# A spectral mixing layer with a cosine-gated MLP on one core: the order of the opening's transfers, and two weight columns fetched through DRAM

## The chip, the cores and the metric

The kernel runs on one core of one Trainium2 chip. The metric is the device time of one execution in microseconds (us). The core's engines are named as in the profile: PE (TensorE, matrix products), DVE (VectorE), ACT (ScalarE), POOL (GpSimd) and SP (SyncE, which here only issues transfers). Everything is in 32-bit floats.

## The reference

`x` has 8 batches of 3008 rows with 256 columns. `w_in` is 256 x 2048 and `w_out` is 2048 x 256.

```
X   = fft(x, over the 3008 rows); X = fft(X, over the 256 columns); a = real(X)
h   = a @ w_in              # 24064 rows, 2048 hidden columns
out = (h * cos(h)) @ w_out
```

## The kernel before, in words

**The transform.** 3008 is 47 x 64. The transform over the rows is made in two stages: a first stage over 47 (`first_half` for the first batch, `pair_half` for the others), whose result `z` is written to DRAM (`store_z`, `store_pair`) and read back in another layout (`load_z`), and a second stage (`second_half`, with the table `BJ`). The transform over the 256 columns is folded into `w_in`: `weights(e, q)` multiplies a quarter q of `w_in` with a cosine (e = 0) or sine (e = 1) table, and `keep_weights` copies the result to `WC` or `WS`. `mix_weights` forms the sums and differences of the raw rows of `w_in` that this needs.

**The row that becomes columns.** The sine of frequency zero is zero, so row 0 of `WS` is free and carries the weights of the alternating column. For each quarter n of the hidden columns, these 512 numbers are needed as four columns of 128, in `wn[:, 4n:4n+4]`. `turn_wn(n)` makes them on PE with four products that have one row and one column (L634), and then has POOL set the row of `WS` to zero (L642). `keep_wn(n)` has DVE copy them out (L645). They are read by `seed` (L694, on ACT), which starts each hidden block's accumulator with `nb * wn + 0.25`; block f of 16 reads column f. So quarter 1 serves blocks 4 to 7, quarter 2 blocks 8 to 11 and quarter 3 blocks 12 to 15.

**The steps.** A step is one batch, one group of about 256 row frequencies (225 in the first group) and one pair of hidden blocks: 8 x 6 x 8 = 384 steps of two halves each. The main loop runs over passes k; pass k starts half k, and does the second product of the step that lies five passes back. In a pass, in this order as far as the opening is concerned:

- `mm1(half, 0)` and `mm1(half, 1)` (L713): the products with `WC` and `WS`; between them ACT copies out the first (`act_e`, L725), and behind them DVE forms the mirrored half (`dve_h`, L729).
- `act_round` (L741, ACT), `dve_frac` (L745, DVE), `act_sin` (L751, ACT), `dve_g` (L755, DVE): h * cos(h), spread over the next passes.
- `sums` (L771, L777, L778, POOL) at pass 2d + 3: sums of the parts of step d, in a tile `S`.
- `mm2` (L804): seven products of step d in place of eight, with blocks of `w_out` and with sums of such blocks. The first three (two with `w_out` itself, one with a sum) come in pass 2d + 5, the fourth at the end of it, the last three in pass 2d + 6.

The sums of blocks of `w_out` are made by POOL in `combine_w2(f0, f1)` (L679, four instructions per pair of blocks) into the tile `VX`. Rows of `w_out` are loaded by `load_w2(f0, f1)` (L254), a quarter (512 KB) at a time. The first step needs the first quarter, (0, 2).

**The opening.** Until the weights are ready, PE makes the first stage of the first batch, and fillers (`keep_busy`, L659). The last six `weights` come within passes 0 to 4. `turn_wn` and `keep_wn` for the quarters 1, 2 and 3 come in passes 1, 3 and 5. What is loaded and combined in which step stands in the dictionary `opening`.

**The queues.** The order on each engine is the order of the program, written out by hand. SP issues nearly all transfers, in its order. In the built program the transfers that SP issues carry eight semaphores in turn, so that each of them waits, before it is issued, for the landing of the one eight places ahead. Two quarters of `w_out`, (0, 2) and (2, 4), are issued by POOL instead, behind its work of pass 1. SP's order around the change, before: the third and fourth quarter of `w_in` with two transfers of `store_z` between them; four more of `store_z`; `load_w2(4, 6)`; `load_bj(256, 512)`; `load_w2(6, 8)`; eight of `load_z` (columns 4 to 8 of z, 32 KB each); the table `L2`; then the second batch's `x`.

**The second batch's x.** `transform(1)` schedules it by steps: `turn_x` (L187, L192; a reversed copy from DRAM to DRAM) in steps 0 and 1, `load_xx` (L210, L217) in steps 1 to 4. POOL reads it first in `take_middle` (L370) from step 8 on.

Of the kernel before, what the change touches and what calls it, by code (L numbers as in the profile page):

```python
# [11 lines left out]
FP = mybir.dt.float32  # L12
# [119 lines left out]
def kernel(  # L132
# [106 lines left out]
    def load_w(q, eng=nc.sync, i0=0, i1=2):  # L239
        eng.dma_start(  # L240
            out=wr[q][:, 512 * i0 : 512 * i1].rearrange("p (i f) -> p i f", f=512),
            in_=moe_w_in[128 * i0 : 128 * i1, 512 * q : 512 * q + 512].rearrange(
                "(i p) f -> p i f", p=128
            ),
        )

    def load_bj(c0, c1, eng=nc.sync):
        eng.dma_start(out=BJ[:, c0:c1], in_=B_dr.ap()[:, c0:c1])
# [4 lines left out]
    def load_w2(f0, f1, eng=nc.sync):  # L253
        eng.dma_start(  # L254
            out=w2.rearrange("p (q c) -> p q c", c=ND)[:, 2 * f0 : 2 * f1],
            in_=moe_w_out.rearrange("(q p) c -> p q c", p=128)[:, 2 * f0 : 2 * f1],
        )
# [210 lines left out]
    def store_z(p, j0=0, j1=NJ, engs=(nc.sync, nc.sync)):  # L468
        half, q = divmod(p, 2)
        zd, zs = take_zd(0, half), zps[p][:, 0:1024]  # L470
        for e in range(2):
            p0 = 16 * e + XP * q
            engs[e].dma_start(
                out=zd[p0 : p0 + XP, 256 * j0 : 256 * j1].rearrange("i (y d) -> y i d", d=128),
                in_=zs[64 * e + 2 * j0 : 64 * e + 2 * j1, :].rearrange("y (i d) -> y i d", d=128),
            )
# [88 lines left out]
    def transform(b):  # L565
        todo = {}

        def at(o, *call):
            todo.setdefault(o, []).append(call)

        for p in range(4):
            sh = (3, 3, 3, 0)[p] if b == 1 else 0
            o = 8 * p + sh
            if p < 2:
                at(p, turn_x, b, p)
            at(1 + p, load_xx, b, p)
            at(5 + p + (3 if b == 1 else 0), take_middle, b, p)
            for k in range(2):
                at(o + 6 + k, fold_x, b, p, k)
                at(o + 9 + k, fold_z, b, p, k)  # L580
            pairs[per * (b - 1) + o + 9] = b, p
            at(o + 11, patch_z, b, p)
            at(o + 12, store_pair, b, p)
            if p == 0:
                for e in range(2):
                    at(4 + 2 * sh + e, fold_ends, e)
                middles.add(per * (b - 1) + o + 10)
                at(o + 12, store_ends, b)
        at(23, load_z, b, 0)
        at(39, load_z, b, 1)  # L590
        for i in range(3):
            doubles[per * (b - 1) + (44, 46, 47)[i]] = b, (2 * i, 2 * i + 1)
        return todo
# [37 lines left out]
    def turn_wn(n, pw):  # L631
        for k in range(4):
            f = 512 * n + 128 * k
            nc.tensor.matmul(  # L634
                pw[:, k : k + 1],
                lhsT=WS[0:1, f : f + 128],
                rhs=ones[0:1, 0:1],
                start=k == 0,
                stop=True,
                skip_group_check=True,  # L640
            )
        nc.gpsimd.memset(WS[0:1, 512 * n : 512 * n + 512], 0.0)  # L642

    def keep_wn(n, pw):
        copy_v(out=wn[:, 4 * n : 4 * n + 4], in_=pw[:, 0:4])  # L645

    class Step:
        pass
# [9 lines left out]
    def keep_busy(pd, n, start):  # L658
        nc.tensor.matmul(  # L659
            pd[:, 0:n],  # L660
            lhsT=VX[:, 0:128],
            rhs=VX[:, 0:n],
            start=start,
            stop=True,
            skip_group_check=True,
        )
# [309 lines left out]
    load_w(2)  # L976
    store_z(2, 4)
    load_w(3)
    keep_busy(pds[0], 512, False)
    pw = [weights(1, 0)]  # L980
    keep_weights(1, 0, pw[0], copy_v)
# [4 lines left out]
    turn_wn(0, pw[0])  # L986
    keep_wn(0, pw[0])
    keep_busy(pds[0], 256, False)
    for p in (0, 3):
        store_z(p, 4)  # L990
    load_w2(4, 6)
    load_bj(256, 512)
    load_w2(6, 8)
    for half in range(2):
        load_z(0, half, 4, 8)
    nc.sync.dma_start(out=L2, in_=L2_dr.ap())
    opening = {
        0: ((load_w2, 2, 4, nc.gpsimd), (combine_w2, 0, 2)),
        1: ((combine_w2, 2, 4),),
        2: ((load_bj, 512, NJ * 64),),  # L1000
        3: ((combine_w2, 4, 6, 0, 2),),
        4: ((combine_w2, 4, 6, 2, 4), (load_z, 0, 0, 8), (load_z, 0, 1, 8)),
        5: ((combine_w2, 6, 8, 0, 2),),
# [32 lines left out]
    for k in range(2 * n + LAG):  # L1036
        t, u = divmod(k, 2)
        d, v = divmod(k - LAG, 2)
        cur, prev, old, nxt = unit(k), unit(k - 1), unit(k - 2), unit(k + 1)
        done = step(d)  # L1040
        full = step(d if v else d - 1, True)
        if cur:
            if k % (2 * per) == 0:
                todo = transform(cur.s.b + 1) if cur.s.b + 1 < NB else {}
            if k >= AHEAD:
                mm1(cur, 0)
                act_e(cur)
            if k == 0:
                for h in (cur, nxt):
                    mm1(h, 0)  # L1050
                    seed_first(h)
                    act_e(h)
                spread_nb(0)
            if k < AHEAD - 1:
                mm1(cur, 1)
        pair = None if u else pairs.pop(t, None)
        double = None if u else doubles.pop(t, None)
        pm = clear_middle() if u and t in middles else None
        if old:
            dve_g(old)  # L1060
            if old.u:
                sums(old.s)
        if done:
            order = (0, 1, 5, 4, 3, 2, 6) if done is steps[-1] else range(7)
            mm2(done, 4 * v, 4 * v + (1 if pair or double else 3), order)
        if pair:
            pz = [borrow("pz"), borrow("pz", 1)]
            for q in range(2):
                pair_half(*pair, q, pz[q])
            mm2(done, 4 * v + 1, 4 * v + 3, order)  # L1070
        if double:
            pbs = [borrow("pb"), borrow("pb", 1)]
            kept = second_half(*double, pbs)
            mm2(done, 4 * v + 1, 4 * v + 3, order)
        if pm is not None:
            middle(pm)
        if full and full is not steps[-1]:
            take_m(full, 1 if v else 3, nc.vector)
        if nxt and 0 < k < AHEAD - 1:
            seed(nxt)  # L1080
        if prev:
            act_round(prev)
        if pm is not None:
            nc.scalar.copy(out=zm, in_=pm)
        if pair:
            keep_z(*pair, 0, pz[0])
        if double:
            keep_b(double[1], kept[0], 0, pbs[0])
        if nxt and k >= AHEAD - 1:
            seed(nxt)  # L1090
        if full and full is not steps[-1]:
            take_m(full, 0 if v else 2, nc.scalar)
        if prev:
            dve_frac(prev)
        if k + 1 in range(2, AHEAD):
            mm1(nxt, 0)
            act_e(nxt)
        if k < 5:
            pw.append(weights(*((1, 1), (0, 1), (1, 2), (0, 2), (1, 3))[k]))
        if k == 4:  # L1100
            pw.append(weights(0, 3))
        if k in (1, 3, 5):
            turn_wn(k // 2 + 1, pw[k + 1])
        copy_small()
        if prev:
            act_sin(prev)
        if pair:
            keep_z(*pair, 1, pz[1])
        if double:
            keep_b(double[1], kept[0], 1, pbs[1])  # L1110
            if double != (0, (1,)):
                send_nb(double[1], *kept)
        if cur and k >= AHEAD - 1:
            mm1(cur, 1)
        if done and v == 0:
            mm2(done, 3, 4, order)
        if cur:
            dve_h(cur)
        if k < 6:
            e, q = ((1, 1), (0, 1), (1, 2), (0, 2), (1, 3), (0, 3))[k]  # L1120
            keep_weights(e, q, pw[k + 2], copy_v)
        if k in (1, 3, 5):
            keep_wn(k // 2 + 1, pw[k + 1])
        if k == 1:
            load_w2(0, 2, nc.gpsimd)
        if k < 2:
            for o in range(2):
                mix_weights(2 + k, o, nc.gpsimd)
        if u == 0:
            continue  # L1130
        for i in range(6):
            s = step(t - 4 - i, True)
            if s:
                combine_m(s, i)
        for sg, lag in ((0, 8), (1, 10)):
            s = step(t - lag, True)
            if s:
                store_out(s, sg)
        for call in opening.pop(t, ()):
            call[0](*call[1:])  # L1140
        for call in todo.pop(t % per, ()):
            call[0](*call[1:])
# [31 lines left out]
```

## Time and profile before

| | |
|---|---|
| three runs before | 1921.13, 1925.23 and 1925.66 us; median 1925.23 us |
| the profiled execution | 1922.86 us, of which the span of the trace is 1921.1 us |
| PE | 1909.9 us busy, 99% of the span |
| ACT, DVE, POOL | 1493.9, 1466.0 and 1443.4 us busy (78, 76 and 75%) |
| transfers | 107.98 MB, mean 56 GB/s; 212 and 158 GB/s in the first two of 40 slices |

Times in the profile are us from the start of the span. A row of the timeline gives the start, the length, the engine, the line of the kernel, what is written from what, the number of instructions merged in it, and in brackets how long the engine had been idle and what released it. SPq and POOLq are the queues from which an engine issues transfers; the length of such a row is the time of the issue, not that of the transfer. One product in 32-bit floats shows as two PE records. Where PE waits, the wait ends the idle time of the next PE row.

### The profile page before, as it was taken

How to read it: one execution, taken by the hardware profiler on the slowest of the kernel's cores; microseconds unless marked ns; L12 is line 12 of the kernel's file. 1: busy time of each engine (PE TensorE's matmuls, PEld its weight loads, DVE VectorE, ACT ScalarE, POOL GpSimd, SP SyncE). 2: the span in 40 equal slices, each digit the busy share in tenths (PEclk: the TensorE clock that was granted, in tenths of full speed). 3: DMA queues.
4: the chain of work that ended last, by engine and by line, in shares of the span. 5: the costliest groups of instructions: out<-in, count | busy, mean ns of one | idle time of the engine just before them, and what ended most of it. 6: DMA issues, size and time to landing. Idle time of an engine off the chain costs nothing.

```text
span 1921.1 us, 32387 instructions
## 1 busy us (share of the span) xinstructions
PE 1909.9 (99%) x10432; PEld 1663.2 (87%) x10432; DVE 1466.0 (76%) x2546; ACT 1493.9 (78%) x3354; POOL 1443.4 (75%) x1784
## 2 busy tenths in 40 slices
PE   9999999999999999999999999999999999999998
PEld 4888888888888889888898888988889888898887
DVE  5777777777777787777777777777777777788787
ACT  3777778777787787777777787778777787788775
POOL 5878868787688876887768786787867887666775
PEclk9999999999999999999999999999999999999999
DMA  7612135022250223412242212512116121200001
GB/s 212 158 24 42 34 63 130 19 38 40 60 118 19 42 42 80 93 23 39 40 111 63 39 26 42 132 40 41 29 34 150 24 40 27 40 24 15 12 15 31
DMA packets 171044, 107.98 MB, mean 56 GB/s; under 512 B 111518, under 2 KB 150268, under 8 KB 169804
## 3 DMA queue, kind: packets, MB, share of 16 engines
q1 hardware_dynamic: 168084, 102.27, 23.8%
q0 software_dynamic: 944, 2.35, 0.4%
q8 instruction: 85, 1.39, 0.3%
q10 hardware_dynamic: 1848, 1.28, 0.3%
q14 instruction: 83, 0.68, 0.1%
HBM read 68.58 MB, written 48.39 MB: 61 GB/s over the span
## 4 chain that ended last, share of the span: by engine, by line
PE 90%; DMA 3%; SPq 3%; POOL 2%; DVE 1%; issue 1%; ACT 0%; DVEq 0%; POOLq 0%
PE M L804 54%; PE H L713 31%; DMA xp<-in_x_dram 2%; PE pz L403 2%; PE pb L521 2%; SPq L210 1%; SPq L942 1%; PE pd L659 1%; POOL xf L377 1%; PE pz L323 0%; DMA xp<-xr 0%; SPq L217 0%; DMA w<-in_moe_w_out_dram 0%; DMA out_dram<-ob 0%; DVE ob L924 0%
## 5 line engine op out<-in xcount | busy, mean ns | idle before, releaser
L771 POOL TENSOR_TENSOR S<-r 128x512 f32<-128x512 f32 (+1 forms) x383 | 474.8, 1240 | 381.0 <-DVE r L755 326.1
L751 ACT ACTIVATE r<-r 128x512 f32<-128x512 f32 (+1 forms) x768 | 476.5, 620 | 246.1 <-DVE r L745 244.6
L745 DVE SCALAR_TENSOR_TENSOR r<-r,H 128x512 f32<-128x512 f32 (+1 forms) x768 | 518.9, 676 | 158.6 <-ACT r L741 133.3
L804 PE MATMUL M<-S,VX 128*128 128x256 f32 (+1 forms) x2304 | 627.5, 378 | 0.0
L755 DVE SCALAR_TENSOR_TENSOR r<-H,r 128x512 f32<-128x512 f32 (+1 forms) x768 | 518.9, 676 | 120.5 <-ACT r L751 76.1
L804 PEld LDWEIGHTS M<-S,VX 128*128 128x128 f32 x2304 | 434.3, 190 | 72.3 <-issue 23.0
L713 PE MATMUL H<-pq,WC 128*128 128x256 f32 (+1 forms) x1536 | 453.1, 377 | 0.4 <-ACT pq L537 0.4
L713 PE MATMUL H<-pq,WS 128*128 128x256 f32 (+1 forms) x1536 | 452.0, 376 | 0.0
L741 ACT ACTIVATE r<-H 128x512 f32<-128x512 f32 (+1 forms) x768 | 447.6, 583 | 0.2 <-DVE H L729 0.2
L729 DVE TENSOR_TENSOR H<-ew,H 128x256 f32<-128x256 f32 (+1 forms) x768 | 325.0, 423 | 153.2 <-PE H L713 93.1
L804 PE MATMUL M<-r,w 128*128 128x256 f32 (+1 forms) x1536 | 387.7, 375 | 0.0
L725 ACT ACTIVATE ew<-H 128x256 f32<-128x256 f32 (+1 forms) x768 | 287.4, 374 | 108.6 <-PE H L713 104.7
L694 ACT ACTIVATE H<-nb,wn 128x256 f32<-128x256 f32 (+1 forms) x766 | 366.0, 478 | 1.9
L804 PEld LDWEIGHTS M<-r,w 128*128 128x128 f32 x1536 | 300.4, 196 | 27.8 <-DVE WS L629 0.9
L713 PEld LDWEIGHTS H<-pq,WC 128*128 128x128 f32 x1536 | 284.1, 190 | 44.7 <-ACT H L694 6.4
L713 PEld LDWEIGHTS H<-pq,WS 128*128 128x128 f32 x1536 | 290.3, 190 | 34.1 <-issue 1.5
L777 POOL TENSOR_TENSOR S<-S,r 128x256 f32<-128x256 f32 (+1 forms) x383 | 275.3, 719 | 30.0
L778 POOL TENSOR_TENSOR S<-r,S 128x256 f32<-128x256 f32 (+1 forms) x383 | 274.8, 718 | 30.0
L804 PE MATMUL M<-r,VX 128*128 128x256 f32 (+1 forms) x768 | 225.8, 376 | 1.9 <-POOL VX L679 1.9
L804 PE MATMUL M<-S,w 128*128 128x256 f32 (+1 forms) x768 | 225.2, 375 | 0.0
L804 PEld LDWEIGHTS M<-S,w 128*128 128x128 f32 x768 | 150.6, 196 | 14.6
L804 PEld LDWEIGHTS M<-r,VX 128*128 128x128 f32 x768 | 146.0, 190 | 16.8 <-POOL VX L679 2.2
(95 smaller groups left out, 893.9 us busy)
## 6 DMA issues: line engine op xcount, KB each, us to landing
out_dram<-ob SPq DMA_DIRECT2D x724, 32.0 KB
xp<-in_x_dram SPq DMA_DIRECT2D x119, 128.0 KB
xp<-xr SPq DMA_DIRECT2D x112, 128.0 KB
z<-zd SPq DMA_DIRECT2D x56, 192.0 KB
xr<-in_x_dram SPq DMA_DIRECT2D x14, 752.0 KB
zd<-zs SPq DMA_DIRECT2D x98, 96.0 KB
nb<-nd SPq DMA_DIRECT2D x23, 256.0 KB
wr<-in_moe_w_in_dram SPq DMA_DIRECT2D x4, 512.0 KB
```

The lines of the kernel that those rows point to most:

```text
L694: nc.scalar.activation(out=h.H[:, 0:T], in_=s.nb[:, 0:T], func=AF.Copy, bias=0.25, scale=wn[:, f : f + 1])
L713: nc.tensor.matmul(h.H[:, 0:T], lhsT=W[:, 128 * f : 128 * f + 128], rhs=s.pq[:, e * 256 : e * 256 + T], start=False, stop=True, skip_group ...
L725: nc.scalar.mul(out=h.ew[:, 0:T], in_=h.H[:, 0:T], mul=2.0)
L729: nc.vector.tensor_tensor(out=h.H[:, T : 2 * T][:, ::-1], in0=h.ew[:, 0:T], in1=h.H[:, 0:T], op=ALU.subtract)
L741: nc.scalar.activation(out=r, in_=y, func=AF.Copy, bias=BIG, scale=1.0)
L745: nc.vector.scalar_tensor_tensor(out=r, in0=r, scalar=-BIG, in1=y, op0=ALU.add, op1=ALU.subtract)
L751: nc.scalar.activation(out=r, in_=r, func=AF.Sin, bias=0.0, scale=SIN_SCALE)
L755: nc.vector.scalar_tensor_tensor(out=r, in0=y, scalar=-0.25, in1=r, op0=ALU.add, op1=ALU.mult)
L771: tt(out=sv[:, 0:2], in0=qv[:, 1:2].to_broadcast([128, 2, T]), in1=qv[:, 0:4:3], op=ALU.subtract,)
L777: tt(out=sv[:, 2], in0=sv[:, 1], in1=gv[:, 0, 0], op=ALU.subtract)
L778: tt(out=sv[:, 3], in0=gv[:, 1, 0], in1=sv[:, 2], op=ALU.add)
L804: nc.tensor.matmul(acc[key][m // 2][:, 256 * (m % 2) : 256 * (m % 2) + T], lhsT=w, rhs=a, start=first, stop=s.fp == 7, skip_group_check=True,)
```

## The change

1. The first two quarters of `w_out`, (0, 2) and (2, 4), are issued by SP right behind the last quarter of `w_in`, and not by POOL. In SP's order they now stand ahead of the last four transfers of `store_z`, of `load_w2(4, 6)`, `load_bj(256, 512)` and `load_w2(6, 8)`. The combination of (2, 4) moves from step 1 to step 2.
2. The columns of `wn` for the quarters 2 and 3 are no longer made on PE. `send_wn(n)` has SP write the row of `WS` (2 KB) to DRAM, and `load_wn(n)` has SP read it back as 128 x 4 single numbers, once the first has landed. `send_wn(2)` stands ahead of the first four of the eight `load_z`, `load_wn(2)` between these and the other four, in pass 2. `send_wn(3)`, `L2` and `load_wn(3)` follow in pass 4. `turn_wn` and `keep_wn` stay for the quarters 0 and 1.
3. The row of `WS` is cleared by `clear_wn(n)` on POOL, in pass 4 (quarter 2) and pass 7 (quarter 3). It waits for `send_wn(n)` to have landed, since that reads the row.
4. The second batch's `turn_x` and first `load_xx` come in step 2; the later ones stay. In SP's order `load_bj(512, ...)` (512 KB) now comes ahead of them.

```
@@ -572,8 +572,8 @@
             if p < 2:
-                at(p, turn_x, b, p)
-            at(1 + p, load_xx, b, p)
+                at(2 if b == 1 else p, turn_x, b, p)
+            at(1 + p if b > 1 else max(2, 1 + p), load_xx, b, p)
@@ -643,6 +643,20 @@
+    wds = {}
+
+    def send_wn(n):
+        wds[n] = dpool.tile([1, 512], FP, tag="wd", bufs=2, name="wd")
+        nc.sync.dma_start(out=wds[n], in_=WS[0:1, 512 * n : 512 * n + 512])
+
+    def clear_wn(n):
+        nc.gpsimd.memset(WS[0:1, 512 * n : 512 * n + 512], 0.0)
+
+    def load_wn(n):
+        nc.sync.dma_start(
+            out=wn[:, 4 * n : 4 * n + 4], in_=wds[n].rearrange("o (k p) -> (o p) k", p=128)
+        )
@@ -976,6 +990,13 @@
     load_w(3)
+    load_w2(0, 2)
+    load_w2(2, 4)
+    for p in (0, 3):
+        store_z(p, 4)
+    load_w2(4, 6)
+    load_bj(256, 512)
+    load_w2(6, 8)
     keep_busy(pds[0], 512, False)
...
@@ -986,18 +1007,9 @@
     keep_busy(pds[0], 256, False)
-    for p in (0, 3):
-        store_z(p, 4)
-    load_w2(4, 6)
-    load_bj(256, 512)
-    load_w2(6, 8)
-    for half in range(2):
-        load_z(0, half, 4, 8)
-    nc.sync.dma_start(out=L2, in_=L2_dr.ap())
     opening = {
-        0: ((load_w2, 2, 4, nc.gpsimd), (combine_w2, 0, 2)),
-        1: ((combine_w2, 2, 4),),
-        2: ((load_bj, 512, NJ * 64),),
+        0: ((combine_w2, 0, 2),),
+        2: ((load_bj, 512, NJ * 64), (combine_w2, 2, 4)),
@@ -1099,8 +1111,8 @@
-        if k in (1, 3, 5):
-            turn_wn(k // 2 + 1, pw[k + 1])
+        if k == 1:
+            turn_wn(1, pw[2])
@@ -1119,10 +1131,20 @@
-        if k in (1, 3, 5):
-            keep_wn(k // 2 + 1, pw[k + 1])
         if k == 1:
-            load_w2(0, 2, nc.gpsimd)
+            keep_wn(1, pw[2])
+        if k == 2:
+            send_wn(2)
+            load_z(0, 0, 4, 8)
+            load_wn(2)
+            load_z(0, 1, 4, 8)
+        if k == 4:
+            send_wn(3)
+            clear_wn(2)
+            nc.sync.dma_start(out=L2, in_=L2_dr.ap())
+            load_wn(3)
+        if k == 7:
+            clear_wn(3)
```

## The prediction

> **What bounds the kernel now.** I read the page's first part first, to see which engine sets the time:
>
> ```profile
> span 1921.1 us, 32387 instructions
> PE 1909.9 (99%) x10432; PEld 1663.2 (87%) x10432; DVE 1466.0 (76%) x2546; ACT 1493.9 (78%) x3354; POOL 1443.4 (75%) x1784
> ```
>
> PE is busy for all but 11.2 us. So what PE wins in the opening stays won at the end, unless a later wait takes it back. Second, busy time by stretches; the columns are the stretch, its length, busy time (and count) of PE, weight loads, DVE, ACT and POOL, then the granted clock, the transfer engines' share and GB/s:
>
> ```profile
> 30.00:32.00 2.00, 2.00 (x10) 0.91 (x12) 1.35 (x3) 0.83 (x3) 0.77 (x1) 1.00 0.94 282
> 32.00:34.00 2.00, 2.00 (x13) 1.17 (x12) 1.31 (x4) 1.67 (x4) 1.81 (x3) 1.00 0.72 242
> 34.00:36.00 2.00, 2.00 (x9) 0.91 (x10) 1.53 (x5) 1.11 (x3) 1.98 (x3) 1.00 0.71 215
> 36.00:38.00 2.00, 2.00 (x10) 0.83 (x10) 2.00 (x5) 1.21 (x4) 2.00 (x3) 1.00 0.99 308
> 38.00:40.00 2.00, 2.00 (x14) 1.60 (x15) 1.75 (x6) 1.30 (x4) 0.49 (x1) 1.00 1.02 366
> 40.00:42.00 2.00, 1.98 (x10) 0.67 (x7) 1.53 (x5) 1.46 (x4) 0.40 (x1) 1.00 1.12 323
> 42.00:44.00 2.00, 0.66 (x4) 0.31 (x2) 0.61 (x2) 0.58 (x1) 1.92 (x4) 1.00 0.79 240
> 44.00:46.00 2.00, 1.44 (x4) 0.90 (x5) 0.00 (x0) 0.00 (x0) 1.92 (x3) 0.61 0.04 14
> 46.00:48.00 2.00, 2.00 (x9) 1.95 (x10) 0.00 (x0) 0.00 (x0) 1.92 (x5) 0.50 0.53 104
> 48.00:50.00 2.00, 2.00 (x7) 1.62 (x6) 1.45 (x4) 0.00 (x0) 1.92 (x4) 0.50 0.87 223
> 50.00:52.00 2.00, 2.00 (x9) 1.86 (x8) 0.77 (x2) 1.60 (x4) 1.92 (x3) 0.68 0.89 303
> ```
>
> PE idles between 42 and 46, and its granted clock is at half from 44.4 (0.61 in the stretch from 44) to 51.3 (0.68 in that from 50). Until then the transfers run nearly without a gap. Third, the chain of waits, which says what PE waited for:
>
> ```profile
> 34.43 7.09 DMA w<-in_moe_w_out_dram
> 44.56 1.12 PE M L804 x2
> 45.68 1.79 PE pw L634 x8
> 47.47 1.05 PE H L713 x2
> 48.52 0.75 PE M L804 x2
> 49.27 0.75 PE H L713 x2
> 50.02 1.83 PE M L804 x6
> 51.85 0.76 PE H L713 x4
> 52.61 1.14 PE M L804 x6
> ```
>
> The first quarter of w_out lands 7.09 us after POOL issued it. POOL then combines it, and only then can PE form the third product of step 0. The same kind of work shows its price at full clock in other rows: 0.19 us for one record of L713 (0.76/4) or of L804 (1.14/6).
>
> **The change part by part.** The places in the timeline that it touches:
>
> ```profile
> 37.71 0.78 POOL L254 DMA_DIRECT2D w<-in_moe_w_out_dram  x1
> 37.76 1.05 PE L634 MATMUL pw<-ones,WS 1*128 1x1 f32 x8
> 38.21 0.43 ACT L694 ACTIVATE H<-nb,wn 128x225 f32<-128x225 f32 x1
> 41.60 1.40 POOL L679 TENSOR_TENSOR VX<-w 128x256 f32<-128x256 f32 x2 [3.11 <-DMA w<-in_moe_w_out_dram]
> 41.65 1.01 PE L804 MATMUL M<-r,w 128*128 128x225 f32 x4
> 44.46 1.06 POOL L771 TENSOR_TENSOR S<-r 128x450 f32<-128x450 f32 x1
> 44.56 1.12 PE L804 MATMUL M<-r,VX 128*128 128x225 f32 x2 [1.90 <-POOL VX L679]
> 53.33 0.46 ACT L694 ACTIVATE H<-nb,wn 128x225 f32<-128x225 f32 x1
> 54.35 0.54 PE L713 MATMUL H<-pq,WC 128*128 128x225 f32 x2
> ```
>
> *turn_wn(2) off PE.* The next product (pass 4) could start 1.0 us earlier (the row at 37.76), but the one behind it needs the seed that ACT ends at 38.64 (38.21 + 0.43). PE resumes there at 38.7 in place of 39.2: 0.5 us won, and step 0's first mm2 can start at 41.1 in place of 41.65.
>
> *First quarter of w_out earlier.* SP asks for it at 29.8 in place of 34.4, 4.7 us earlier. With the same 7.09 us it lands at 36.9 in place of 41.5. POOL ended mix_weights just before 37.71, where it issued the second quarter; rid of the first issue (0.8 us, as this one) it ends at about 37.0, and its combination at 39.9 (2.9 us, as from 41.60 to 44.5), ahead of the 41.9 at which PE asks. The 1.9 us wait goes, and if the wait causes the half clock, that goes too.
>
> *turn_wn(3) off PE.* Removed with its 1.79 us. Together: from 41.65 to 51.85 (10.2 us), PE did 18 records of L713 and L804 beside turn_wn(3): 4 in the row at 41.65, then 2 + 2 + 2 + 2 + 6. At 0.19 they take 3.42 us. So pass 6's last product starts at 41.1 + 3.42 = 44.5 in place of 51.85: **7.3 us won**, made of 0.5 (the start), 1.9 (wait), 1.8 (turn_wn) and 3.1 (half clock).
>
> *The new waits.* Now blocks 8 to 11 hang on two transfers in a row, which stand behind the whole of w_out in SP's queue. Its rows now, and those of a small transfer to DRAM alone on the queue, of a small read of z that POOL issued (the "to landing" row), of the second batch's last x and of its last first-reader:
>
> ```profile
> 29.77 1.04 SPq L473 DMA_DIRECT2D zd<-zs  x1
> 35.74 0.43 SPq L254 DMA_DIRECT2D w<-in_moe_w_out_dram  x1
> 45.10 0.30 SPq L506 DMA_DIRECT2D z<-zd  x1
> 45.92 0.64 SPq L187 DMA_DIRECT2D xr<-in_x_dram  x1
> 101.75 0.70 SPq L545 DMA_DIRECT2D nd<-pq  x1
> 103.51 0.34 SPq L549 DMA_DIRECT2D nb<-nd  x1
> DMA to landing us min/median/max: 1.9/2.1/2.2
> 79.28 0.31 SPq L210 DMA_DIRECT2D xp<-xr  x1
> 95.59 0.49 POOL L370 TENSOR_TENSOR xm<-xp 64x4 f32<-64x4 f32 x2
> ```
>
> The eighth load_z went out at 45.10 because it waits for the last quarter of w_out (eight places ahead, issued at 35.74): that landed at 45.0. When does send_wn(2) land? From 30 to 44 the transfers moved 2 x (282 + 242 + 215 + 308 + 366 + 323 + 240) = 3950 KB. After the change all of it stands ahead of send_wn(2) but the eight load_z (256 KB), so 3690 KB, which the same rates move by 42.9. If the dip from 32 to 36 fills up to 282, it is 42.0. The last landing came 1.0 us behind the data before (45.0 against 44). So send_wn(2) lands between 43.0 and, if it also takes the 1.76 us of the nd transfer behind the data, 44.7; I take 44.2, as it lies right behind the last quarter.
>
> load_wn(2) then reads 512 single numbers; no transfer of that kind is in the trace. Below, it takes the 2.1 us of the small z reads, and nothing speaks for less. Above, it takes the 7.09 of 512 KB in a full queue. I take 3.0, near the lower end, because the queue is empty then (14 GB/s from 44 to 46). So the columns land at 44.2 + 0.1 + 3.0 = 47.3. ACT wants them for block 8's seed at 53.33 - 7.2 = 46.1 and PE its result at 54.35 - 7.2 = 47.15. The seed ends at 47.8: **PE waits 0.6 us** (none at the lower end, 4.7 at the upper). Behind that seed on ACT queue the sine of half 6 and the rounding of the next half; PE's products reach both two or more passes later.
>
> The Trainium skill, "DMA: Bandwidth & Descriptors", section "Rules for kernel authors", says that a strided last dimension becomes one descriptor per element, which speaks against this read; it gives no price for it, and no run here shows one yet.
>
> *clear_wn(2) on POOL.* It waits for send_wn(2), and step 1's sums queue behind it: 44.2 + 0.5 (the memset), then the sums: 1.06 for the first, as at 44.46, and an estimated 1.4 for the two of half its width. The first is there at 45.8, and PE asks at 46.8 (five products behind 44.9, where pass 6 ends). The combination of (2, 4) takes another 2.9, to 50.1, and PE asks for it at 50.2 (fourteen products behind 44.9). So it costs about 0.2, and each us by which send_wn(2) lands later costs up to one. clear_wn(3) finds its transfer landed (four load_z and 1.8 us behind load_wn(2), about 48.5, when POOL reaches it at 52.6): nothing. load_wn(3) lands by 52; block 12's seed is due at 54. Nothing.
>
> *The rest.* load_z waits on PE no sooner than pass 12, at 63.6 - 7 = 56, and is there by 49. The x of the second batch starts behind load_wn(3) and 512 KB of BJ, 3 to 5 us later than 45.92. SP ends it at 83 to 84 in place of 79.6, and POOL reads the last of it at 95.59 - 7 = 88.5. That cover of 4 us hides it; without it POOL would wait, and then PE.
>
> **The sum.** 7.3 - 0.6 - 0.2 = 6.5 us. On the profiled execution (1922.86) that gives 1916.4. This lies 2.4 below the median of the runs (1925.23); of the four times that I have, the middle is 1924.0. I forecast 1924.0 - 6.5 = **1917.5 us**.
>
> **The clock, by row and by rule.** PE was idle for 1.9 us (42.66 to 44.56), and the clock fell at its end, for 6.9 us. The Trainium skill, "TensorE: Matmul & The Clock Gate", Part 1, says that the clock falls after at least one idle window of about 3.4 us. By that rule this wait alone is too short, and the trace does not agree with it in length, though the fall to half it shows.
>
> **The rivals.**
> - *The half clock stays* (chance 0.07). Not the wait but the thin work before it (64-column weights, one-row products) may lower it. For it: the wait is short. Against it: the same work ran from 30 to 38 at 1.00. The 18 records then run on at half: 7.3 - 3.1 - 0.8 (the new waits) = 3.4 us won, 1920.6.
> - *A new wait takes most of it* (0.28). The columns land 2 us or more too late (a read of 4.4 us), or send_wn(2) lands at 46. For it: two landings in a row, and the queue's last was 9.3 us old (35.74 to 45.0). Against: the empty queue. A wait of 2 us, as before, again with half clock (3.1): 7.3 - 2 - 3.1 = 2.2 us won, 1921.8.
> - *Slower than before* (0.11). One mechanism: the read of 512 single numbers is slow. The point where it decides is a wait of 7.3 - 3.1 = 4.2 us, a read of 6.6 us; at 12 us it is 7.3 - 9.6 - 3.1, so 5.4 slower, 1929.4.
> - *The quarter lands no earlier* (0.04). If the queue is bound by bytes and shares them out, it lands at 41 as before, and only the two turn_wn go: 2.3 us won, 1921.7. Against: SP's order puts it first.
>
> **How the numbers follow.** My forecast case (6.5, from 5 to 7.5) has 0.50: 1916 to 1919, and 2 us either way for the spread of runs. 0.3% is 5.8 us, about what a measurement of this kernel can tell from no change. My case lies over it in about 0.42 of its 0.50. Faster 0.44: that and a little of the others. Same 0.44: the rest, the half clock, the new wait and the unmoved quarter. Slower 0.12. The range from 1914 to 1924 takes in these but the slow tail.
>
> **What would show it.** PE's row of M<-r,VX at about 42 without a wait for VX; granted clock 1.00 in all stretches from 42 to 52; two turn_wn of eight records gone; the first row of block 8 (L713) at 47 to 48; POOL's clear waiting for a transfer until 44; the second batch's last x issued at 83. It is wrong if ACT's seed waits for a transfer beyond 48, or the clock is at half somewhere in 40 to 55.

## The result and the profile after

The changed kernel took 1919.04 us (median of 15 runs, 1916.16 to 1922.76). The kernel before took 1922.45 us (15 runs, 1921.13 to 1925.66). The ratio is 0.998, interval 0.9972 to 0.9988: 3.4 us less. That is 0.2%, below the 0.3% that the prediction takes for the limit of such a measurement, but the interval does not reach 1. The two profiled executions lie further apart: the span fell from 1921.1 to 1914.9 us. Why these two differences are not the same is the question of the experiments.

The first part of the profile after, span and busy time:

```profile
span 1914.9 us, 32358 instructions
PE 1904.7 (99%) x10416; PEld 1658.3 (87%) x10416; DVE 1464.4 (76%) x2544; ACT 1493.7 (78%) x3354; POOL 1441.1 (75%) x1782
```

PE's idle time is 10.2 us, 1.0 less than before: the wait of 1.9 us is gone, and 0.9 us are back as small waits elsewhere in the opening. The other 5.2 us are busy time: 1.8 and 1.0 us are the two removed `turn_wn` at their prices in the profile before, and the rest is left for products that ran at half clock there.

Busy time by stretches after, with the columns as before (length; PE, weight loads, DVE, ACT and POOL; granted clock; share of the transfer engines; GB/s):

```profile
42.00:44.00 2.00, 2.00 (x12) 1.99 (x11) 1.21 (x3) 0.69 (x2) 1.54 (x4) 1.00 0.73 249
44.00:46.00 2.00, 2.00 (x13) 1.94 (x12) 1.69 (x5) 1.65 (x5) 1.84 (x3) 1.00 0.27 39
46.00:48.00 2.00, 2.00 (x12) 1.99 (x11) 1.70 (x4) 1.55 (x4) 2.00 (x4) 1.00 0.35 102
...
50.00:52.00 2.00, 2.00 (x12) 2.00 (x11) 1.65 (x3) 1.65 (x5) 1.84 (x4) 1.00 0.85 204
```

The hole in PE between 42 and 46 and the half clock behind it are gone. The chain of waits in the same place:

```profile
41.36 1.35 PE M L818 x6
...
43.85 1.14 PE M L818 x6
44.99 0.76 PE H L727 x4
```

No transfer and no POOL stands in it. The row of four records of L727 is pass 6's last product with its neighbour; before it stood at 51.85. I use it as a marker. The marker moved by 6.9 us. What lies behind it differs little: span minus marker is 1869.25 us before and 1869.91 after. So nearly all that the change does to the time, it does in the first 52 us. The 0.7 us lost behind the marker do not look like chance: the kernels below that fetch the columns through DRAM need 1869.9 to 1870.5 us there, the others 1869.4 to 1869.5. (The price of the read and the early x, which disturb the marker itself, are left out of this.) Where they are lost stays open.

The timeline after, at the places that the change touches (SPq is SP's queue, with the time of the issue):

```profile
37.42 1.43 POOL L693 TENSOR_TENSOR VX<-w 128x256 f32<-128x256 f32 x2
...
39.58 0.31 SPq L651 DMA_DIRECT2D wd<-WS  x1
...
41.29 1.03 PE L818 MATMUL M<-r,w 128*128 128x225 f32 x4
42.16 0.55 PE L818 MATMUL M<-r,VX 128*128 128x225 f32 x2
...
43.22 0.38 SPq L657 DMA_DIRECT2D wn<-wd  x1
43.25 0.51 POOL L654 MEMSET WS<- 1x512 f32 x1 [0.38 <-DMA wd<-WS]
...
46.52 0.46 ACT L708 ACTIVATE H<-nb,wn 128x225 f32<-128x225 f32 x1
46.73 0.54 PE L727 MATMUL H<-pq,WS 128*128 128x225 f32 x2
```

PE starts the first products of step 0 at 41.29. POOL combines the first quarter at 37.42 without waiting for it, and PE's product with VX stands at 42.16 without a wait. The first send of the row lands at about 43.2, where POOL's clear and the read behind it start. ACT's seed of block 8 (46.52) and PE's product for that block (46.73) wait for nothing.

### The profile page after: what moved, and what is told of

Its sections match the earlier page's. It is cut to its first block, busy times and chain, and to the rows that moved or that the text cites. A ratio compares the mean times of both kernels' runs of the same rounds, so it can differ in the third digit from the quotient of the medians.

```text
span 1914.9 us, 32358 instructions
## 1 busy us (share of the span) xinstructions
PE 1904.7 (99%) x10416; PEld 1658.3 (87%) x10416; DVE 1464.4 (76%) x2544; ACT 1493.7 (78%) x3354; POOL 1441.1 (75%) x1782
## 4 chain that ended last, share of the span: by engine, by line
PE 90%; DMA 4%; SPq 3%; POOL 1%; DVE 1%; issue 0%; ACT 0%; DVEq 0%; ACTq 0%; POOLq 0%
PE M L818 55%; PE H L727 31%; DMA xp<-in_x_dram 3%; PE pz L403 2%; PE pb L521 2%; SPq L210 1%; SPq L956 1%; DMA out_dram<-ob 0%; SPq L217 0%; POOL xf L377 0%; PE pw L618 0%; DVE ob L938 0%; PE pz L323 0%; PE pm L456 0%; DVE r L769 0%
## 5 line engine op out<-in xcount | busy, mean ns | idle before, releaser
L727 PE MATMUL H<-pq,WC 128*128 128x256 f32 (+1 forms) x1536 | 452.8, 376 | 0.8 <-ACT pq L537 0.5
L727 PE MATMUL H<-pq,WS 128*128 128x256 f32 (+1 forms) x1536 | 451.4, 375 | 0.0
L727 PEld LDWEIGHTS H<-pq,WC 128*128 128x128 f32 x1536 | 283.5, 190 | 45.7 <-ACT H L708 7.2
L727 PEld LDWEIGHTS H<-pq,WS 128*128 128x128 f32 x1536 | 289.9, 190 | 35.3 <-issue 1.5
```

Source lines behind the costliest of these rows:

```text
L727: nc.tensor.matmul(h.H[:, 0:T], lhsT=W[:, 128 * f : 128 * f + 128], rhs=s.pq[:, e * 256 : e * 256 + T], start=False, stop=True, skip_group ...
```

## The experiments

Three theories were open once the profiles were compared. The first is the prediction's: the 1.9 us wait lowers the clock, so both go together and the gain is about 6 us in every run. A rival: the half clock is drawn anew in each execution, from what PE does in the whole opening, and the change removes only one of the places where it can fall, so the certain gain is what is left without the clock. A second rival: one half of the change does all of it, and the other is hidden anyway.

**The changed kernel again.** No edit; a second profile and five runs beside the kernel before.

> The changed kernel once more, for a second profiled execution. Theory A (the wait for w_out's first quarter cost 1.9 us and half clock for another 3.1; both are gone): the profile again shows no wait for VX and the clock at 1.00 from 42 to 52 us, and the times lie 3 to 6 us below the kernel before. Theory C (the runs of the changed kernel spread from 1916.2 to 1922.8 because a stretch of half clock, 6 to 7 us long, falls into some executions and not into others): if this execution takes 1918.5 us or more, its trace shows such a stretch somewhere, at a place where the first profile had 1.00, and its length times one half is the difference to 1914.9. Rival D (the spread is spread over the whole run, as many small waits): no such stretch, and PE's idle time is larger instead.

Measured: 1917.38 us (1916.62 to 1918.44), before 1923.68 (27 runs), ratio 0.9966 (0.9952 to 0.998); 6.3 us less this time. Its profile has a span of 1916.7 us, 1.8 more than the first. The stretches of that profile:

```profile
28.00:30.00 2.00, 2.00 (x9) 1.33 (x8) 1.13 (x2) 1.08 (x4) 0.00 (x0) 0.91 0.82 287
30.00:32.00 2.00, 2.00 (x6) 0.29 (x4) 0.40 (x1) 0.98 (x2) 0.00 (x0) 0.50 1.07 341
32.00:34.00 2.00, 2.00 (x8) 1.15 (x8) 1.50 (x3) 0.26 (x2) 1.49 (x2) 0.74 1.03 355
```

Here the changed kernel has a half clock, at another place. Its length follows from the clock column: 0.91 in the first stretch is 0.36 us at half, 0.50 is all 2 us, 0.74 is 1.04 us; together 3.4 us. It costs half of that, 1.7 us, and the marker stands at 46.64, 1.65 later than in the first profile of the same kernel. PE's only idle time in the ten microseconds ahead of it is one of 0.46 us, and the first profile has the same one at the same place; PE's row in the first profile and then in this one:

```profile
26.76 0.65 PE L727 MATMUL H<-pq,WC 128*128 128x225 f32 x2 [0.46 <-ACT pq L537]
```

```profile
26.82 0.65 PE L727 MATMUL H<-pq,WC 128*128 128x225 f32 x2 [0.46 <-ACT pq L537]
```

The clock fell after the second and not after the first.

**The order of w_out alone.** The kernel before, with the first two quarters asked for by SP and everything else as it was:

```diff
     load_w(3)
+    load_w2(0, 2)
+    load_w2(2, 4)
...
-        0: ((load_w2, 2, 4, nc.gpsimd), (combine_w2, 0, 2)),
+        0: ((combine_w2, 0, 2),),
...
-        if k == 1:
-            load_w2(0, 2, nc.gpsimd)
```

> Only the order of w_out's first two quarters from the change; the columns are made on PE as before, x as before. Theory A: no wait for VX, clock 1.00 from 42 to 52 us; of the 7.3 us only the two turn_wn at full clock stay (0.5 and 1.0), so 5.8 us of span are won against the 1921.1 before: about 1915.3. Rival B (the thin work ahead of the wait lowers the clock, not the wait): the clock falls to half near 44 all the same, and only the 1.9 us of the wait are won: about 1919.

Measured: 1920.71 us (1918.65 to 1922.35, 11 runs), ratio 0.9985 (0.9977 to 0.9994). Its timeline, PE's rows:

```profile
42.32 1.04 PE L804 MATMUL M<-r,w 128*128 128x225 f32 x4
43.20 0.54 PE L804 MATMUL M<-r,VX 128*128 128x225 f32 x2
...
46.47 1.00 PE L804 MATMUL M<-S,VX 128*128 128x225 f32 x4 [0.41 <-DVE wn L645]
```

The wait for VX is gone with this part alone, and the granted clock of this profile is 1.00 in all of the opening. Its span is 1917.3 us, 2.0 more than theory A has it. What stays is `turn_wn(3)`, in the chain of waits of this kernel:

```profile
43.74 0.98 PE pw L634 x8
...
47.85 0.76 PE H L713 x4
```

At full clock it takes 0.98 us (1.79 in the profile before, where the clock was at half), and behind it PE waits 0.41 us for DVE's copy of the column. The marker stands at 47.85, 2.9 behind that of the changed kernel. Of this, 1.0 us stands already at step 0's first products (42.32 against 41.29): `turn_wn(2)`, and an opening that was 0.6 us late before it. From there to the marker this kernel takes 5.53 us and the changed one 3.70, both at full clock. So `turn_wn(3)` with all that hangs on it is worth 1.8 us: its own 0.98, the wait of 0.41, and 0.4 in the rows around them.

**The columns and the later x alone.** The changed kernel, with the first two quarters of w_out on POOL as before:

```diff
-    load_w2(0, 2)
-    load_w2(2, 4)
...
-        0: ((combine_w2, 0, 2),),
+        0: ((load_w2, 2, 4, nc.gpsimd), (combine_w2, 0, 2)),
...
+        if k == 1:
+            load_w2(0, 2, nc.gpsimd)
```

> The columns of the last two quarters over DRAM and x later, as changed, but w_out's first two quarters issued by POOL as before. Theory A: the wait for VX stays and is longer by what turn_wn(2) took (2.0 to 2.9 us), the clock falls to half near 44 again; only turn_wn(3) is won, 1.8 us, less what the columns cost at half clock: 1919 to 1921 of span. Rival B (thin work): turn_wn gone from the stretch ahead, so the clock stays at 1.00 and about 5 us are won: 1916.

Measured: 1921.06 us (1919.51 to 1922.34, 11 runs), ratio 0.9988 (0.9979 to 0.9997). The wait is there, to the hundredth of a microsecond as in the kernel before, in the timeline:

```profile
44.41 0.65 PE L818 MATMUL M<-r,VX 128*128 128x225 f32 x2 [1.90 <-POOL VX L693]
```

But the clock did not fall. One row for the stretch from 42 to 52 says it best; first the kernel before, then this one:

```profile
42.00:52.00 10.00, 8.10 (x28) 6.64 (x27) 2.82 (x7) 2.18 (x5) 9.61 (x14) 0.66 0.62 177
```

```profile
42.00:52.00 10.00, 8.10 (x41) 7.24 (x40) 5.53 (x11) 5.04 (x12) 9.53 (x15) 1.00 0.57 147
```

PE is busy for 8.10 us in both, with the same wait in front, and does 28 records in one and 41 in the other. So the wait alone does not decide the clock. The rival of thin work expected this much of the clock, since `turn_wn(2)` is gone from the work ahead of the wait. But in the run above `turn_wn(2)` was there, the wait was not, and the clock stayed at 1.00 as well; so the thin work alone does not decide it either. Each of these is one profile, and whether it takes both together these two cannot tell.

**The wait filled.** The kernel before, with four products of 256 columns that nobody reads, in PE's queue just ahead of the product with VX; extra work that the reference does not need:

```diff
+            if k == LAG:
+                mm2(done, 0, 2, order)
+                pf = borrow("pd", 1)
+                for i in range(4):
+                    nc.tensor.matmul(
+                        pf[:, 0:256], lhsT=CS[:, 0:128], rhs=CS, start=i == 0,
+                        stop=True, skip_group_check=True,
+                    )
+                mm2(done, 2, 3, order)
+            else:
-            mm2(done, 4 * v, 4 * v + (1 if pair or double else 3), order)
+                mm2(done, 4 * v, 4 * v + (1 if pair or double else 3), order)
```

> The kernel before, with four products of 256 columns (nobody reads their result) between the second and the third product of step 0, that is in PE's wait for VX; each takes about 0.43 us, 1.7 us in all. Theory A: PE is no longer idle, the clock stays at 1.00 from 44 to 51, and 2.8 to 3.3 us are won though work was added: span 1918. Rival B: the clock falls all the same, and the time is that of before or up to 0.3 us more.

Measured: 1922.58 us (1920.72 to 1923.89, 11 runs), ratio 0.9994 (0.9985 to 1.0003). The fillers took 1.7 us in place of the wait, and the clock was 1.00 from 44 to 50, as theory A expects. The 3 us that it expects to be won were not. In the same profile it was at half earlier, by the stretches:

```profile
28.00:30.00 2.00, 2.00 (x5) 1.29 (x5) 1.07 (x2) 0.36 (x1) 0.00 (x0) 0.50 0.90 288
30.00:32.00 2.00, 2.00 (x5) 0.87 (x4) 0.00 (x0) 1.16 (x3) 0.00 (x0) 0.50 0.99 303
32.00:34.00 2.00, 2.00 (x6) 0.38 (x5) 0.40 (x1) 0.55 (x1) 1.85 (x2) 0.50 0.69 228
34.00:36.00 2.00, 2.00 (x8) 1.15 (x8) 1.53 (x3) 0.58 (x2) 0.68 (x1) 0.79 0.70 206
```

Worked out as above that is 6.84 us, twice the stretch of the changed kernel's second profile, and as long as the one of the profile before (44.44 to 51.28). This one stands where the edit has changed nothing.

**The earlier gap filled.** The changed kernel, with one unused product of 256 columns in PE's idle time at 26.3, where it waits 0.46 us for ACT:

```diff
+    pf = psum("pd", "M")
+    nc.tensor.matmul(pf[:, 0:256], lhsT=CS[:, 0:128], rhs=CS, start=True, stop=True)
```

> The changed kernel with one product of 256 columns more (0.43 us, its result is read by nobody), where PE waits 0.46 us at 26.3 for ACT's copy of the first transformed group. Theory C (what is left of the spread is a clock at half for one or two stretches of 3.4 us, released by the thin work and the wait between 24 and 30 us; it came in one of two profiles of the changed kernel): the product costs nothing, since it lies in the wait, the stretch at half comes less often, and the median falls from 1917.4 to 1919.0 towards 1917 us. Rival D (the spread has another origin): the times stay as they are, or rise by up to 0.4 us.

Measured: 1918.47 us (1917.58 to 1919.79, 7 runs), ratio 0.9973 (0.9962 to 0.9983). There is no half clock in the opening of its profile, but the marker stands at 46.23, 1.2 later than in the changed kernel's first, since `turn_wn(0)`, ahead of the gap, began 1.2 later as well (25.24 against 24.00). The seven runs lie within 2.2 us, against 6.6 for the first fifteen of the changed kernel and 1.8 for its second five, and the time is no better.

**More idle time.** The changed kernel without one filler of 512 columns ahead of `turn_wn(0)`; work that no result needs is left out:

```diff
-    keep_busy(pds[0], 512, False)
```

> The changed kernel without the second filler of 512 columns (1.05 us at 23.0). The second stage of the first group waits for z, which lands no sooner, so PE is idle for about 1.0 us more between 22 and 27. Theory C: the clock falls to half near 28 in most executions, and the median rises by 1.5 to 3 us though work was taken away. Rival D: no change, or up to 0.5 us faster.

Measured: 1921.64 us (1920.4 to 1922.51, 11 runs), ratio 0.9989 (0.998 to 0.9998): slower than the changed kernel by 2.6 us of the medians, with less work. PE's rows in the timeline, and the first and last of the stretches with a lower clock:

```profile
26.29 0.91 PE L521 MATMUL pb<-BJ,z 64*64 64x64 f32 x32 [0.81 <-DMA z<-zd]
27.58 0.65 PE L727 MATMUL H<-pq,WC 128*128 128x225 f32 x2 [0.38 <-ACT pq L537]
```

```profile
28.00:30.00 2.00, 2.00 (x9) 1.24 (x8) 1.35 (x2) 0.36 (x1) 0.00 (x0) 0.93 0.98 317
...
36.00:38.00 2.00, 2.00 (x13) 0.98 (x9) 0.69 (x1) 1.23 (x3) 0.00 (x0) 0.86 0.90 293
```

Short idle times that add to 1.2 us are followed by a half clock from 29.72 to 36.56, with 0.50 in all the stretches between: 6.84 us.

These kernels differ in how often the half clock falls. Each run comes with its mean granted clock, rounded to 0.001; one stretch of 3.4 us at half is 1.7 us of 1920, so 0.0009 of it. The mean also counts the end of the execution: in all eleven profiles PE has nothing left to do in the last 5.6 to 5.8 us, and the clock is at half in the last 1.1 to 3.7 us (from 1912.4 in the changed kernel's first profile). A stretch of 6.8 us is 0.0018 and the end at least 0.0003, so a run at 0.999 or more has had no such stretch in its opening. But it can have had one of 3.4; the sorting is rough. Sorted by that (the kernel before: its runs beside the experiments; the changed one: its 15 runs and the 5 of the first experiment):

| kernel | runs | at 0.999 or more | their median, us | median of those at 0.998 |
|---|---|---|---|---|
| before | 63 | 6 | 1920.97 | 1923.29 |
| before, wait filled | 11 | 6 | 1921.44 | 1923.63 |
| order of w_out alone | 11 | 5 | 1919.05 | 1920.19 (1 run) |
| columns and later x alone | 11 | 2 | 1920.16 | 1921.28 |
| changed | 20 | 9 | 1917.25 | 1919.93 |
| changed, gap filled | 7 | 5 | 1917.99 | 1919.51 |
| changed, more idle | 11 | 0 | none | 1920.86 |
| changed, x of the second batch as before (below) | 11 | 1 | 1925.57 | 1925.93 |
| before, later x alone (below) | 10 | 1 | 1919.48 | 1921.55 |

At equal clock, as far as the sorting goes, the change is worth 3.7 us (1920.97 - 1917.25), the order of w_out alone 1.9 (1920.97 - 1919.05), the columns and the later x alone 0.8, on two runs. So neither half does all of it. Filling the wait won nothing at equal clock, as it must, since the fillers take the wait's time; but 6 of 11 runs instead of 6 of 63 stayed at 0.999 or more, and with more idle time none of 11 did. So idle time goes with how often the clock falls for long; it does not tell whether it falls in a given run. (The counts are small, and the kernels differ in more than their idle time.)

**The price of the read.** The changed kernel, with a copy of the four columns by DVE at the end of pass 5, which nobody reads; it is there to make an engine wait for the read:

```diff
+        if k == 5:
+            copy_v(out=seen, in_=wn[:, 8:12])
```

> The changed kernel with a copy of the four columns of quarter 2 on DVE at the end of pass 5, as soon as they are asked for, so that the trace shows when the read of 512 single numbers lands. My estimate was 3.0 us from the issue at 43.2: DVE then waits until 46.2, about 2 us, and PE a little. If the read takes as little as the small reads of z (2.1), it ends at 45.3; at 7 us the wait would end at 50 and the time rise by 4 us or more. Against the spread of the seeds in the first profile (ACT's seed of block 8 ran at 46.52 without waiting) it can be no more than 3.3.

Measured in one run: 1919.36 us, span 1917.6. The chain of waits runs through both transfers:

```profile
39.38 5.10 DMA wd<-WS
44.48 0.02 issue
44.49 2.09 DMA wn<-wd
46.59 0.02 issue
46.61 0.23 DVE seen L1148
```

The send of 2 KB behind the whole of w_out takes 5.1 us here (3.6 in the changed kernel's first profile, 39.58 to 43.22), the read of 512 single numbers 2.1 us. PE then waited 1.67 us (behind DVE and ACT), once more without a fall of the clock. The columns landed at 46.59. Set beside the first profile, whose step 0 began 0.24 us earlier, ACT's seed would have wanted them at about 46.8: the margin is there, but here it is only about 0.2 us.

**The x of the second batch as before.** The changed kernel, with this one part undone:

```diff
-                at(2 if b == 1 else p, turn_x, b, p)
-            at(1 + p if b > 1 else max(2, 1 + p), load_xx, b, p)
+                at(p, turn_x, b, p)
+            at(1 + p, load_xx, b, p)
```

> The changed kernel with the second batch's x asked for as early as before (turn_x in steps 0 and 1, load_xx in steps 1 to 4). My prediction costed the later x at nothing: the median is that of the changed kernel, 1917 to 1919.5, and SP's transfers of x end some 3 us earlier. Rival: the earlier x stands in SP's queue ahead of the columns of quarter 3 or of z and delays them, and PE's row of block 12 waits; then 1 to 4 us slower.

Measured: 1926.81 us (1925.45 to 1928.24, 11 runs), ratio 1.0016 (1.0007 to 1.0025), span 1925.0: slower than the kernel before, and 8.3 us slower than the changed one at equal clock, a figure that rests on its one run at 0.999 (1925.57). The rival in the expectation had 1 to 4 us. The timeline around the second send:

```profile
52.86 1.82 SPq L217 DMA_DIRECT2D xz<-in_x_dram  x4
54.72 0.57 SPq L192 DMA_DIRECT2D xr<-in_x_dram  x1
55.82 0.23 SPq L651 DMA_DIRECT2D wd<-WS  x1
...
59.55 0.38 SPq L657 DMA_DIRECT2D wn<-wd  x1
59.59 0.52 POOL L654 MEMSET WS<- 1x512 f32 x1 [5.74 <-DMA wd<-WS]
...
61.78 0.46 ACT L708 ACTIVATE H<-nb,wn 128x225 f32<-128x225 f32 x1 [4.92 <-DMA wn<-wd]
...
62.54 1.12 PE L818 MATMUL M<-S,VX 128*128 128x225 f32 x2 [5.04 <-POOL S L785]
```

The x of the second batch stands ahead of the second send in SP's queue, so that goes out at 55.82; with the later x it went out at 45.97. POOL's clear waits 5.74 us for it, the sums of a step queue behind the clear, and PE waits 5.04 us for the sums. A half clock from 61.0 to 67.9 follows; another one, from 30.3 to 33.7, stands ahead of all this. The later x is thus what makes the columns through DRAM affordable.

**The later x alone.** The kernel before, with that part alone (the lines above, the other way round).

> The kernel before with one edit alone: the second batch's x in the order of the changed kernel (turn_x from step 2 on, load_xx from step 2 on). Theory A, the later x is worth nothing by itself, it only keeps SP's queue free for the two sends of the row: the wait of about 1.9 us for the first combined quarter stays, pass 6's last product starts at about 51.9 with a half clock behind the wait or 48.5 without one, no engine waits for x at 83 to 96, and the time is that of the kernel before within 1 us: 1921.5 to 1923.5 as a median, ratio 0.9995 to 1.0005. Rival, the later x has a price of its own: POOL waits for xp at about 90 to 96, PE behind it, and the time is 1 to 3 us above the kernel before, 1924 to 1926. Second rival, it has a gain of its own, because the transfers of x no longer run beside the reads of z or the table BJ: 2 us or more below, 1920.5 or less.

Measured: 1922.44 us (1919.48 to 1925.48, 10 runs), before 1922.57 (13 runs), ratio 1.0001 (0.9991 to 1.0011). Theory A holds, with one difference: the wait was not there in this profile. The stretches and PE's rows:

```profile
28.00:30.00 2.00, 2.00 (x6) 1.18 (x6) 1.33 (x2) 0.36 (x1) 0.00 (x0) 0.66 0.87 297
...
34.00:36.00 2.00, 2.00 (x8) 1.36 (x8) 1.53 (x3) 0.09 (x1) 0.88 (x1) 0.64 0.69 204
```

```profile
46.53 0.65 PE L804 MATMUL M<-r,VX 128*128 128x225 f32 x2
47.10 1.05 PE L634 MATMUL pw<-ones,WS 1*128 1x1 f32 x8
...
49.90 1.00 PE L804 MATMUL M<-S,VX 128*128 128x225 f32 x4 [0.41 <-DVE wn L645]
```

A half clock of 6.8 us (28.64 to 35.44) delayed PE and, behind PE, POOL: PE's first products of step 0 start at 45.52 in place of 41.65, and POOL asked for the first quarter at 38.38 in place of 34.43. But the quarter then landed 5.2 us after its issue, not 7.1, and so in time. The marker stands at 51.29, as good as the 51.85 of the profile before. In the kernel before, a half clock ahead of the wait is paid for in part by the wait; in the changed one nothing is left to pay with.

## Why the prediction was right, and where not

The forecast was 1917.5, the median 1919.04, inside the range and 1.5 us above. By its steps:

- *The first quarter earlier: right.* POOL combined it from 37.42 to 40.3, against 39.9 for the end, and PE's product with VX stands at 42.16. The order of w_out alone removes the whole wait, and at equal clock it is worth 1.9 us. The rival by which the quarter lands no earlier falls.
- *turn_wn(2), 0.5 us: about right.* Step 0's first product of `mm2` starts at 41.29 in place of 41.65, and PE waits for ACT's seed until 38.84 (38.7 in the forecast).
- *turn_wn(3), 1.8 us: the size is right, by luck.* The row was priced at half clock, and the clock's part of it was not sure to be won. At full clock the row costs 0.98 us, but 0.41 us of wait for DVE's copy, which the profile before did not show, and 0.4 us around them make up for it: 1.8 us between the order of w_out alone and the changed kernel.
- *The half clock, 3.1 us: the term that failed.* I counted it as a sure gain, on "if the wait causes the half clock, that goes too". The columns alone had the same 1.90 us wait at full clock, and the changed kernel itself had a half clock elsewhere, from 29.6 to 33.0. It is a matter of odds: 6 of 63 runs before and 9 of 20 after kept a mean clock of 0.999 or more. Without it the sum is 0.5 + 1.9 + 1.8 = 4.2 us at the marker, and 3.5 with the 0.7 us that are lost behind the marker, which the prediction did not have; at equal clock 3.7 are measured. The pair of profiles shows 6.2 because a run before with 6.8 us at half met a run after with none in its opening.
- *The new waits, 0.8 us: none came.* In the first profile the send landed at 43.2, near the lower end (43.0), not at 44.2; in the one with the price of the read it landed at 44.5, near the upper end (44.7). The read took 2.1 us, the lower end, not 3.0; with 3.0 the columns would have been there at 47.5 in that profile, 0.7 us after they were wanted. Columns and first row of block 8 (46.73) came in time, and the clear held POOL up for 0.38 us before a sum that PE did not wait for. The rivals by which a new wait or a slow read decides fall with the read's 2.1 us.
- *clear_wn(3) and load_wn(3) at nothing: right*, but only as long as SP's queue is free for the second send.
- *The later x at nothing: right as a cost, incomplete as a step.* The last of it was issued by 83.2 and POOL read it at 88.75 without waiting. By itself it is worth nothing (1.0001). I did not ask what would stand in SP's queue ahead of the second send without it: 8.3 us. A late row, the mechanism of the rival that ends slower, is what happens then, with the queue as its cause in place of the read.

The win was forecast at 6.5 us. It came out at 3.4 in the first comparison, 6.3 in the second (1923.68 - 1917.38), and 5.2 between the medians of all runs here, from several sessions (1923.37 for 78 before, 1918.14 for 20 after). About 3.7 of it do not hang on the clock; the rest is the clock, which falls for long less often in the changed kernel and not, as the prediction had it, in every run before and in none after. That 0.8 us of waits did not come made up for a part. The forecast time is nearer to the first median than the win is, by luck: its base, 1924.0, lay 1.5 us above the median of the 15 runs before.

The Trainium skill, "TensorE: Matmul & The Clock Gate", Part 1, says that the clock gate watches a free-running window of about 3.4 us, and that the count of slow products at a kernel's start varies from run to run with the window's phase. The stretches at half here, 3.4 and 6.8 us long, agree with such a window, and so does a fall that comes in one execution and not in the next. The ends of the profiles point the same way: PE's last products are alike in all of them and nothing follows, yet the clock falls 2.0 us behind them in the run with the early x (1919.3 to 1921.3) and 4.6 us in the one with the price of the read (1911.9 to 1916.5). The table of the same part of the Trainium skill has the half clock come after at least one idle window. That does not agree with the openings here: a half clock followed 1.90 us of idle time in the profile before, and 0.46 us, in a stretch of thin work, in the changed kernel's second profile. What makes a window count as idle stays open, and so does the phase as the cause: the runs show the odds, and a delay that varies, not the phase.

## What to carry to other kernels

A half clock seen in one profile is one draw: take a second profile, sort the runs by mean clock (knowing what else the mean counts), and sum a change at full-clock prices before adding the clock as a chance. When a small transfer becomes a dependency, ask what stands ahead of it in its queue, for each time it is sent; here a part of the change that by itself does nothing was worth 8 us to another part. A wait that is removed also removes the slack that used to absorb earlier delays. To price a part, compare the way between two marks in two kernels at full clock, not the one row that goes.

## What the hardware showed that was not expected

In the openings profiled here the half clock comes in stretches of one length or twice that: 3.4 us (29.6 to 33.0 in the changed kernel's second profile, 30.3 to 33.7 with the early x) and 6.8 us (in the profile before, with the wait filled, with more idle time, with the early x, and with x later). At the end, where PE has nothing left to do, the clock fell 2.0 to 4.6 us behind PE's last product, at another moment in each profile. A read of 512 single numbers from DRAM into 128 partitions, with little else moving (23 GB/s from 44.5 to 46.6), took 2.09 us, no more than the 2.1 us median of the small read of z that the prediction quotes. A send of 2 KB into DRAM behind a full queue took 3.6 us in one profile and 5.1 us in another.
